# Moving the low part of the queries and the norm steps from VectorE to GpSimd, with half-height query loads and paired negations, in a fused attention and two-MLP kernel

## The chip, the cores and the metric

One core of one Trainium2 chip runs the whole program in one launch. The metric is device time in microseconds (us), the median over the runs. The engines have the names of the profile: PE is TensorE (PEld its weight loads), DVE is VectorE, ACT is ScalarE, POOL is GpSimd, and SP is SyncE, whose queue issues all of this kernel's DMAs.

## The reference

Inputs are q, k, v of shape (4, 12, 448, 64), so S = 448 and D = 64, and the weights of two feed-forward blocks over 1792 tokens of width 768.

```python
def rmsnorm(x, g):
    rms = np.sqrt(np.mean(x * x, axis=-1, keepdims=True) + 1e-06)
    return x / rms * g
q_n, k_n = rmsnorm(q, g_q), rmsnorm(k, g_k)
scores = (1.0 / np.sqrt(64)) * np.matmul(q_n, k_n.transpose(0, 1, 3, 2))
scores = scores - np.max(scores, axis=-1, keepdims=True)
attn = np.exp(scores)
attn = attn / (np.sum(attn, axis=-1, keepdims=True) + 1e-09)
x = np.matmul(attn, v)                # then heads side by side: (1792, 768)
x = ((x @ w1) * (x @ w2) @ w3) @ w_out
h = x @ w_in
out = (h * np.clip(h + 3.0, 0.0, 6.0) / 6.0) @ w_out2
```

## The kernel before, in words

The 48 heads are taken as 24 pairs (NP = 24). Everything is float32, and accuracy comes from splitting: a value is copied to the rounded type that PE multiplies quickly (the high part, on ACT), the rest is found by a subtraction (the low part, on DVE or POOL), and PE multiplies both.

A pair goes through attention in eight steps, one for each block of 112 queries (four) of each of its two heads. One turn of the main loop (lines 721 to 749) is one step. In step t it emits the two score matmuls of step t (L536, L537), the exponential of step t - 1 (`expo`, L555, ACT), the transposes of the exponentials of the pair before (`trans`, L562), their low part (`tlo`, L581, DVE), then `scale_max` (L543, DVE: scales the scores and takes the row maximum) and `negate` (L550, DVE: one column of the maximum times -1, as the bias of the exponential), the copy of the high part (`thi`, L571, ACT), and the product with the values (L602 to L615).

The queries of a pair are loaded twice, one copy above the other, into 128 partitions of the tile qr, 896 columns (`load_q`, one buffer). `qhi` (L505, ACT) scales all 128 rows by the product G of the two norm weights and writes the rounded result to the tile Q. `qlo` (L510, DVE) then turns rows 64 to 127 of Q into the low part: qr times G, less Q. `ksplit` writes the keys' high part on ACT (L516) and their low part on POOL (L517). The score matmul contracts over all 128 partitions, so high and low queries are summed in one pass.

The norms are taken for two pairs at a time. `ssq` (L436, ACT) squares, `ssum` (L442, DVE) adds up, `rms1` takes mean plus epsilon (L448, DVE) and then a logarithm and an exponential (L450, L451, ACT), and `rms2` does one Newton step and the factor 1/8 (L460 to L464 and L466, five small DVE instructions on 112 x 32 and 112 x 16). The result for the keys goes through two transposes and through HBM (rkd) to come back as a broadcast row (rb). At the end of a pair `rsum1` (L634, L635, DVE) inverts the sums, and `xout` (L639, POOL) multiplies the output by them once they are back from HBM as rsb.

Beside this run fillers, paced by `fill(*rate(t))`: first the product of w3 and w_out (to about 240 us), then the layers of the first feed-forward block. A preparation of weights feeds them: a load (raw), a conversion from the float64 bit pattern (L135 on ACT, L136, L138 and L141 on DVE), a high copy on ACT (L201, L285), and a low part on POOL (L203, L287), which frees the raw buffer for the next load. A part of a filler is placed behind the anchors of two or three steps ago (score, maximum and exponential).

The order on each engine is decided when the program is built: functions are entered at step times (lines 681 to 719, moved by SHIFT), and a scheduler with a modelled timeline orders the instructions. On the chip every engine and the SP queue then works strictly in that order.

Of the kernel before, what the change touches and what calls it, by code (L numbers as in the profile page):

```python
# [12 lines left out]
F32 = mybir.dt.float32  # L13
# [3 lines left out]
AF = mybir.ActivationFunctionType  # L17
ALU = mybir.AluOpType
# [4 lines left out]
B, H, S, D = 4, 12, 448, 64  # L23
HP = H // 2
NP = B * HP
P = 128
# [20 lines left out]
def fused_kernel(ctx: ExitStack, tc: tile.TileContext, nat, qT, kT, vin, gq, gk,  # L47
                 w12, w3t, wo, win, wo2, outT):
    nc = tc.nc
# [15 lines left out]
    G = gs[:, 2:3]  # L65
# [21 lines left out]
    def dma(out, src):  # L87
        return nc.sync.dma_start(out, src)
# [313 lines left out]
    T = {}  # L402
    anchors = {}

    def attention(ap, rate):
# [10 lines left out]
                    dma(T["nat", i], nat[i].rearrange("p a b d -> p (a b) d"))  # L416

        def load_q(i):
            T["qr", i] = ap.tile([P, 2, S], F32, tag="qr", bufs=1, name="qr")
            dma(T["qr", i], qT[i])  # L420

        def load_k(i):
            T["kr", i] = ap.tile([P, 2, S], F32, tag="kr", bufs=1, name="kr")
# [14 lines left out]
        def ssum(i, g):  # L438
            x = T.pop(("nat", i))
            if i == g[0]:  # L440
                T["ss", g[0]] = ap.tile([CP, 2, len(g), 2 * NC], F32, tag="ss", bufs=2, name="ss")
            nc.vector.reduce_sum(T["ss", g[0]][:, :, i - g[0], :],  # L442
                                 x.rearrange("p (a b) d -> p a b d", a=2), axis=AX.X)

        def rms1(g):
            w = 16 * len(g)
            v = T["ss", g[0]].rearrange("p a b c -> p (a b c)")
            nc.vector.tensor_scalar(v, v, 1.0 / D, 1e-6, op0=ALU.mult, op1=ALU.add)  # L448
            y = ap.tile([CP, w], F32, tag="ry", bufs=2, name="ry")
            nc.scalar.activation(y, v, AF.Ln)  # L450
            nc.scalar.activation(y, y, AF.Exp, scale=-0.5)  # L451
            T["ry", g[0]] = y

        def rms2(g):
            n = len(g)
            w = 16 * n
            v = T.pop(("ss", g[0])).rearrange("p a b c -> p (a b c)")
            y = T.pop(("ry", g[0]))
            t = ap.tile([CP, w], F32, tag="rt", bufs=2, name="rt")
            nc.vector.tensor_mul(t, y, y)  # L460
            nc.vector.tensor_mul(t, t, v)
            nc.vector.tensor_scalar(t, t, -0.5, 1.5, op0=ALU.mult, op1=ALU.add)
            r = ap.tile([CP, w], F32, tag="rr", bufs=2, name="rr")
            nc.vector.tensor_mul(r, y, t)  # L464
            rq = ap.tile([CP, n, 8], F32, tag="rq", bufs=3, name="rq")
            nc.vector.tensor_scalar_mul(rq, r[:, : 8 * n].rearrange("p (a b) -> p a b", b=8), 0.125)  # L466
            for i in g:
                T["rq", i] = rq[:, i - g[0], :]
            T["rr", g[0]] = r
# [32 lines left out]

        def qhi(i):
            T["Q", i] = q = ap.tile([P, 2, S], F32R, tag="Q", bufs=2, name="Q")
            nc.scalar.activation(q, T["qr", i], AF.Copy, scale=G)  # L505

        def qlo(i):
            a = slice(64, 128)
            q = T["Q", i]
            nc.vector.scalar_tensor_tensor(out=q[a], in0=T["qr", i][a], scalar=G[a, :], in1=q[a],  # L510
                                           op0=ALU.mult, op1=ALU.subtract)

        def ksplit(i):
            k1, k2 = T["K", i] = [ap.tile([P, 2, S], F32R, tag=f"K{z}", bufs=2, name="K") for z in range(2)]
# [12 lines left out]
        def score(i, s):  # L527
            j, c = divmod(s, NC)
            if s == 0:
                T["PP", i] = ap.tile([CP, NC, 2 * S], F32, tag="PP", bufs=2, name="PP")  # L530
                T["m", i] = ap.tile([CP, 16], F32, tag="mx", bufs=2, name="mx")
                T["sum", i] = ap.tile([CP, 8], F32, tag="sum", bufs=2, name="sum")
            k1, k2 = T["K", i]
            ps = bank("s")
            qs = T["Q", i][:, j, c * CP : c * CP + CP]
            nc.tensor.matmul(ps[:CP, :S], qs, k1[:, j, :], start=True, stop=False)  # L536
            anchors[8 * i + s] = [nc.tensor.matmul(ps[:CP, :S], qs, k2[:, j, :], start=False, stop=True)]  # L537
            return ps
# [8 lines left out]

        def negate(i, s):
            m = T["m", i]
            nc.vector.tensor_scalar_mul(m[:, 8 + s : 9 + s], m[:, s : s + 1], -1.0)  # L550

        def expo(i, s):
            j, c = divmod(s, NC)
            v = T["PP", i][:, c, j * S : j * S + S]
            anchors[8 * i + s].append(nc.scalar.activation(  # L555
                v, v, AF.Exp, bias=T["m", i][:, 8 + s : 9 + s], accum_out=T["sum", i][:, s : s + 1]))

        def trans(i, kb):
            src = T["PP", i]
            ps = bank("t")  # L560
            for c in range(NC):
                nc.tensor.transpose(ps[:, c * CP : c * CP + CP], src[:, c, kb * P : kb * P + P],  # L562
                                    ident[:CP, :CP])
            hi = ap.tile([P, S], F32 if full(i) else F32R, tag="xh", bufs=3, name="xh")
            lo = None if full(i) else ap.tile([P, S], F32R, tag="xl", bufs=3, name="xl")
            T["X", i, kb] = (ps[:, :S], hi, lo)
# [9 lines left out]
        def tlo(i, kb):  # L576
            ps, hi, lo = T["X", i, kb]
            if full(i):
                return
            if kb != 3 or i < K3:  # L580
                nc.vector.tensor_sub(lo, ps, hi)  # L581
            else:
                nc.vector.tensor_sub(hi[64:128, :], ps[0:64, :], hi[0:64, :])
                nc.vector.tensor_sub(lo[0:64, :], ps[64:128, :], lo[64:128, :])
# [96 lines left out]
        for i in range(NP):  # L681
            t = 8 * i
            n = i + 1
# [9 lines left out]
            if i % 2 == 0 and i + 2 < NP:  # L693
                g = groups[i + 2]
# [19 lines left out]
            if i % 2 == 0 and i + 2 < NP:  # L714
                g = groups[i + 2]
# [5 lines left out]
        t = -1  # L721
        while t < 8 * NP + 22 or xs_ready:
            t += 1
            if t == 4:
                first.close()
            now[0] = t
            live = t < 8 * NP
            ps = score(*divmod(t, 8)) if live else None
            if 0 < t <= 8 * NP:
                expo(*divmod(t - 1, 8))  # L730
            u = t - LG
            if 0 <= u < 8 * NP and u % 8 < 7:
                trans(*divmod(u, 8))
            if 0 <= u - 1 < 8 * NP and (u - 1) % 8 < 7:
                tlo(*divmod(u - 1, 8))
            if live:
                scale_max(t // 8, t % 8, ps)
                negate(*divmod(t, 8))
            if 0 <= u < 8 * NP and u % 8 < 7:
                thi(*divmod(u, 8))  # L740
            if 0 <= u - 2 < 8 * NP and (u - 2) % 8 < 7:
                pv(*divmod(u - 2, 8))
            with ExitStack() as es:
                for a in anchors.get(t - (3 if "pool" in L else 2), ()):
                    es.enter_context(tc.issue_after(a.ins))
                fill(*rate(t))
            run_tasks()
            if "pool" in L:
                xnext()

    def rate(t):
        if "pool" not in L:
            return 1.05, 2
        if L["cur"] < 8:
            return 2.5, 4
        return 1.6, 2
# [48 lines left out]
    step, q = 0, 0  # L805
# [33 lines left out]
    for b, t in enumerate(order):  # L839
        acc = None  # L840
        for m in range(M2):
# [26 lines left out]
            if acc is None:  # L868
# [4 lines left out]
                                           op0=ALU.min, op1=ALU.mult)  # L873
            g = lp.tile([P, 2, S], F32R, tag="g", bufs=2, name="g")
# [57 lines left out]
```

## Time and profile before

| what | value |
|---|---|
| median of 3 runs | 1273.02 us (1271.57 to 1277.7) |
| the profiled execution | 1276.18 us, span 1274.3 us |
| busy over the span | PE 93%, PEld 81%, DVE 62%, ACT 53%, POOL 36% |
| mean granted clock of PE | 0.968 of full |
| DMA | 203.72 MB, mean 160 GB/s |
| chain that ended last | PE 67%, DMA 11%, DVE 10%, issue 5%, ACT 3%, POOL 2% |

The shares are means over stages that differ: attention with the weight product, to about 240 us; attention with the first feed-forward block, to about 640 us; the rest of that block; and from about 870 us the second block alone, in which PE is busy throughout from 900 to 1200 us. So the stage tables, not the shares, say what a change in one stage is worth. In the rows, L12 is line 12 of the kernel, and a releaser behind an arrow is what ended the idle time of an engine.

### The profile page before, as it was taken

How to read it: one execution, taken by the hardware profiler on the slowest of the kernel's cores; microseconds unless marked ns; L12 is line 12 of the kernel's file. 1: busy time of each engine (PE TensorE's matmuls, PEld its weight loads, DVE VectorE, ACT ScalarE, POOL GpSimd, SP SyncE). 2: the span in 40 equal slices, each digit the busy share in tenths (PEclk: the TensorE clock that was granted, in tenths of full speed). 3: DMA queues.
4: the chain of work that ended last, by engine and by line, in shares of the span. 5: the costliest groups of instructions: out<-in, count | busy, mean ns of one | idle time of the engine just before them, and what ended most of it. 6: DMA issues, size and time to landing. Idle time of an engine off the chain costs nothing.

```text
span 1274.3 us, 16884 instructions
## 1 busy us (share of the span) xinstructions
PE 1183.1 (93%) x5868; PEld 1033.9 (81%) x5868; DVE 795.1 (62%) x1524; ACT 678.8 (53%) x1305; POOL 463.6 (36%) x292
## 2 busy tenths in 40 slices
PE   3587998888889999999999999889999999999998
PEld 2355987667668999999998998778999999999997
DVE  6989789989993578768643446994433343343332
ACT  5887667866783566766642223444533353344332
POOL 4334324624443112222111003445454454545542
PEclk9698998989999999999999999899999999999999
DMA  7898664666688666676349983450100020001001
GB/s 248 253 256 243 202 193 167 194 229 228 211 274 306 209 217 199 235 225 220 134 163 382 348 323 113 158 173 25 60 28 1 1 87 1 1 1 44 1 1 44
DMA packets 64693, 203.72 MB, mean 160 GB/s; under 512 B 8544, under 2 KB 25440, under 8 KB 64608
## 3 DMA queue, kind: packets, MB, share of 16 engines
q1 hardware_dynamic: 64608, 202.65, 48.2%
q8 instruction: 46, 0.75, 0.2%
q14 instruction: 39, 0.32, 0.1%
HBM read 173.93 MB, written 28.68 MB: 159 GB/s over the span
## 4 chain that ended last, share of the span: by engine, by line
PE 67%; DMA 11%; DVE 10%; issue 5%; ACT 3%; POOL 2%; SPq 1%; DVEq 0%; POOLq 0%; ACTq 0%
PE bank L80 8%; PE bank L82 8%; PE bank L81 8%; PE acc L81 6%; PE acc L82 6%; PE acc L80 5%; PE h L80 5%; PE h L81 5%; PE h L82 5%; PE bank L562 3%; DMA raw<-in_w_dram 2%; DVE wf L141 2%; DMA wr<-in_wo_dram 2%; PE bank L536 2%; PE bank L537 2%
## 5 line engine op out<-in xcount | busy, mean ns | idle before, releaser
L800 POOL TENSOR_TENSOR wis<-wf,wis 128x768 fp32r<-128x768 f32 x63 | 119.8, 1902 | 234.1 <-ACT wis L799 234.1
L872 DVE SCALAR_TENSOR_TENSOR u<-u,h 128x448 f32<-128x448 f32 x64 | 39.5, 618 | 217.3 <-ACT u L871 217.3
L800 POOL TENSOR_TENSOR wos<-wf,wos 128x768 fp32r<-128x768 f32 x64 | 119.0, 1860 | 103.6 <-ACT wos L799 103.6
L80 PE MATMUL bank<-xhl,ws 128*128 128x448 f32 x384 | 145.1, 378 | 7.7 <-ACT ws L285 6.3
L543 DVE CUSTOM_DVE_ANT_0 PP<-bank,rb,rq 112x448 f32<-112x448 f32 x192 | 129.1, 677 | 31.9 <-PE bank L537 27.4
L82 PE MATMUL bank<-xhl,ws 128*128 128x448 f32 x384 | 143.9, 375 | 4.9 <-POOL ws L287 4.9
L81 PE MATMUL acc<-g,wos 128*128 128x448 f32 x384 | 144.3, 376 | 3.8 <-DVE g L876 3.7
L555 ACT ACTIVATE PP<-PP,mx 112x448 f32<-112x448 f32 x192 | 127.4, 664 | 37.4 <-DVE mx L550 34.2
L80 PE MATMUL acc<-g,wos 128*128 128x448 f32 x384 | 138.5, 371 | 5.5 <-ACT g L875 5.5
L82 PE MATMUL acc<-g,wos 128*128 128x448 f32 x384 | 143.2, 373 | 0.0
L81 PE MATMUL bank<-xhl,ws 128*128 128x448 f32 x384 | 142.5, 371 | 0.1
L80 PE MATMUL h<-x2h,wis 128*128 128x448 f32 x378 | 139.0, 368 | 0.0
L81 PE MATMUL h<-x2h,wis 128*128 128x448 f32 x378 | 138.9, 368 | 0.0
L82 PE MATMUL h<-x2h,wis 128*128 128x448 f32 x378 | 137.5, 364 | 0.4 <-POOL wis L800 0.4
L876 DVE TENSOR_TENSOR g<-u,g 128x448 fp32r<-128x448 f32 x64 | 97.9, 1529 | 33.6 <-ACT g L875 33.6
L871 ACT ACTIVATE u<-h,half 128x448 f32<-128x448 f32 x64 | 40.4, 631 | 143.2 <-PE h L82 143.2
L536 PE MATMUL bank<-K,Q 128*112 128x448 f32 x192 | 78.3, 409 | 37.5 <-DVE mx L543 25.0
L562 PE MATMUL bank<-ident,PP 112*128 112x112 f32 x672 | 97.0, 267 | 11.8 <-DVE xl L581 10.2
L562 PEld LDWEIGHTS bank<-ident,PP 112*128 112x128 f32 x672 | 80.5, 145 | 33.8 <-DVE xl L581 13.3
L571 ACT ACTIVATE xh<-bank 128x448 fp32r<-128x448 f32 (+1 forms) x156 | 83.0, 537 | 43.3 <-PE bank L562 38.4
L581 DVE TENSOR_TENSOR xl<-bank,xh 128x448 fp32r<-128x448 f32 x142 | 87.1, 615 | 25.5 <-ACT xh L571 23.8
L799 ACT ACTIVATE wos<-wf 128x768 fp32r<-128x768 f32 x64 | 54.1, 846 | 86.9 <-PE acc L82 86.7
(126 smaller groups left out, 2763.5 us busy)
## 6 DMA issues: line engine op xcount, KB each, us to landing
ws<-w12d SPq DMA_DIRECT2D x48, 768.0 KB, 5.1
ws<-wpd SPq DMA_DIRECT2D x32, 768.0 KB, 4.2
raw<-in_w_dram SPq DMA_DIRECT2D x32, 384.0 KB, 4.3
w12d<-ws SPq DMA_DIRECT2D x16, 768.0 KB, 6.0
wr<-in_win_dram SPq DMA_DIRECT2D x16, 768.0 KB, 4.5
wr<-in_wo_dram SPq DMA_DIRECT2D x16, 768.0 KB, 6.6
nat<-in_nat_dram SPq DMA_DIRECT2D x24, 448.0 KB, 5.9
qr<-in_qT_dram SPq DMA_DIRECT2D x24, 448.0 KB, 6.4
```

The costliest lines, as they stand in the source:

```text
L80: nc.tensor.matmul(ps, lh, rh, start=first, stop=False)
L81: nc.tensor.matmul(ps, lh, rl, start=False, stop=False)
L82: return nc.tensor.matmul(ps, ll, rh, start=False, stop=last)
L536: nc.tensor.matmul(ps[:CP, :S], qs, k1[:, j, :], start=True, stop=False)
L543: anchors[8 * i + s].append(nc.vector.tensor_tensor_reduce(out=T["PP", i][:, c, sl], in0=ps[:CP, :S], in1=T["rb", i][:, sl], op0=ALU.mult, ...
L555: anchors[8 * i + s].append(nc.scalar.activation(v, v, AF.Exp, bias=T["m", i][:, 8 + s : 9 + s], accum_out=T["sum", i][:, s : s + 1]))
L562: nc.tensor.transpose(ps[:, c * CP : c * CP + CP], src[:, c, kb * P : kb * P + P], ident[:CP, :CP])
L571: nc.scalar.activation(hi, ps, AF.Copy)
L581: nc.vector.tensor_sub(lo, ps, hi)
L799: nc.scalar.activation(t[:, 0, :], wf[q], AF.Copy)
L800: nc.gpsimd.tensor_sub(t[:, 1, :], wf[q], t[:, 0, :])
L876: nc.vector.tensor_sub(g[:, 1, :], u, g[:, 0, :])
```

## The change

Four edits. The queries are loaded to 64 partitions, scaled there in place by ACT, and copied to the upper half of Q by a second ACT instruction; the low part is a POOL subtraction. The six small steps of `rms1` and `rms2` run on POOL for every group but the first. `negate` works in odd steps only, on two columns. The exponential of step t - 2, not t - 1, is emitted in step t.

```diff
         def load_q(i):
-            T["qr", i] = ap.tile([P, 2, S], F32, tag="qr", bufs=1, name="qr")
-            dma(T["qr", i], qT[i])
+            T["qr", i] = ap.tile([D, 2, S], F32, tag="qr", bufs=1, name="qr")
+            dma(T["qr", i], qT[i][:D])
...
+        def eng(g):
+            return nc.gpsimd if g[0] else nc.vector
+
         def rms1(g):
...
-            nc.vector.tensor_scalar(v, v, 1.0 / D, 1e-6, op0=ALU.mult, op1=ALU.add)
+            eng(g).tensor_scalar(v, v, 1.0 / D, 1e-6, op0=ALU.mult, op1=ALU.add)
...
-            nc.vector.tensor_mul(t, y, y)
-            nc.vector.tensor_mul(t, t, v)
-            nc.vector.tensor_scalar(t, t, -0.5, 1.5, op0=ALU.mult, op1=ALU.add)
+            eng(g).tensor_mul(t, y, y)
+            eng(g).tensor_mul(t, t, v)
+            eng(g).tensor_scalar(t, t, -0.5, 1.5, op0=ALU.mult, op1=ALU.add)
             r = ap.tile([CP, w], F32, tag="rr", bufs=2, name="rr")
-            nc.vector.tensor_mul(r, y, t)
+            eng(g).tensor_mul(r, y, t)
             rq = ap.tile([CP, n, 8], F32, tag="rq", bufs=3, name="rq")
-            nc.vector.tensor_scalar_mul(rq, r[:, : 8 * n].rearrange("p (a b) -> p a b", b=8), 0.125)
+            eng(g).tensor_scalar_mul(rq, r[:, : 8 * n].rearrange("p (a b) -> p a b", b=8), 0.125)
...
         def qhi(i):
             T["Q", i] = q = ap.tile([P, 2, S], F32R, tag="Q", bufs=2, name="Q")
-            nc.scalar.activation(q, T["qr", i], AF.Copy, scale=G)
+            qr = T["qr", i]
+            nc.scalar.activation(qr, qr, AF.Copy, scale=G[:D, :])
+            nc.scalar.activation(q[:D], qr, AF.Copy)
 
         def qlo(i):
-            a = slice(64, 128)
             q = T["Q", i]
-            nc.vector.scalar_tensor_tensor(out=q[a], in0=T["qr", i][a], scalar=G[a, :], in1=q[a],
-                                           op0=ALU.mult, op1=ALU.subtract)
+            nc.gpsimd.tensor_sub(q[D:], T["qr", i], q[:D])
...
         def negate(i, s):
             m = T["m", i]
-            nc.vector.tensor_scalar_mul(m[:, 8 + s : 9 + s], m[:, s : s + 1], -1.0)
+            if s % 2:
+                nc.vector.tensor_scalar_mul(m[:, 7 + s : 9 + s], m[:, s - 1 : s + 1], -1.0)
...
-            if 0 < t <= 8 * NP:
-                expo(*divmod(t - 1, 8))
+            if 1 < t <= 8 * NP + 1:
+                expo(*divmod(t - 2, 8))
```

## Rows read from the trace of the kernel before

**Rows 1.** Stretches: length, busy PE, PEld, DVE, ACT, POOL (count), clock, DMA share, GB/s.
```profile
40.00:400.00 360.00, 305.76 (x1500) 243.79 (x1499) 320.68 (x767) 263.16 (x574) 150.99 (x109) 0.91 0.72 223
...
400.00:480.00 80.00, 80.00 (x434) 72.64 (x433) 43.43 (x104) 41.41 (x87) 11.53 (x8) 1.00 0.67 225
```

**Rows 2.** The longest wait of PE, 40 to 400 us: total us, times, longest us.
```profile
PE bank L536 <- DVE mx L543: 20.9, 12, 5.8
```

**Rows 3.** Groups on DVE, 40 to 400 us: busy us, mean ns | idle before.
```profile
L510 DVE SCALAR_TENSOR_TENSOR Q<-qr,gs,Q 64x896 fp32r<-64x896 f32 x14 | 23.2, 1660 | 2.5 <-ACT Q L505 2.1
...
L550 DVE TENSOR_SCALAR mx<-mx 112x1 f32<-112x1 f32 x107 | 14.9, 142 | 0.4
...
L460 DVE TENSOR_TENSOR rt<-ry 112x32 f32<-112x32 f32 x11 | 5.1, 464 | 0.1
L462 DVE TENSOR_SCALAR rt<-rt 112x32 f32<-112x32 f32 x11 | 4.8, 439 | 0.0
...
L448 DVE TENSOR_SCALAR ss<-ss 112x32 f32<-112x32 f32 x10 | 3.1, 308 | 0.0
...
L461 DVE TENSOR_TENSOR rt<-rt,ss 112x32 f32<-112x32 f32 x11 | 2.9, 261 | 0.1
...
L466 DVE TENSOR_SCALAR rq<-rr 112x16 f32<-112x16 f32 x9 | 2.3, 257 | 0.0
```

**Rows 4.** The same stretch, line L464 alone: its busy us and count.
```profile
40.00:400.00 360.00, 2.11 (x9) 0.91 0.72 223
```

**Rows 5.** The chain that ended last, to 420 us: start us, us, what.
```profile
41.79 1.15 DVE Q L510
43.02 1.84 issue
...
53.20 1.82 DVE rt L462
...
181.73 2.17 issue
...
203.45 2.44 issue
...
360.86 1.16 DVE Q L510
```

**Rows 6.** Timelines of DVE and of POOL: start us, us, what, idle before.
```profile
181.70 2.17 DVE L510 SCALAR_TENSOR_TENSOR Q<-qr,gs,Q 64x896 fp32r<-64x896 f32 x1 [1.83 <-ACT Q L505]
...
180.80 2.12 POOL L517 TENSOR_TENSOR K<-kr,K 128x896 fp32r<-128x896 f32 x1 [7.77 <-ACT K L516]
```

**Rows 7.** Single lines of the whole run: duration ns least/median/longest, first and last start.
```profile
L510 DVE SCALAR_TENSOR_TENSOR Q<-qr,gs,Q x24: 1150/1635/3026, 10.1 to 595.6; 64x896 fp32r<-64x896 f32 x24
...
L550 DVE TENSOR_SCALAR mx<-mx x192: 130/147/156, 22.4 to 640.4; 112x1 f32<-112x1 f32 x192
...
L634 DVE TENSOR_SCALAR sum<-sum x24: 151/172/1244, 44.9 to 641.4; 112x8 f32<-112x8 f32 x24
...
L141 DVE SCALAR_TENSOR_TENSOR raw<-raw x64: 535/556/1634, 14.6 to 383.4; 128x384 int32<-128x384 int32 x48, 128x512 int32<-128x512 int32 x16
```

**Rows 8.** More groups, 40 to 400 us: POOL and ACT, then DVE.
```profile
L517 POOL TENSOR_TENSOR K<-kr,K 128x896 fp32r<-128x896 f32 x14 | 31.2, 2232 | 22.8 <-ACT K L516 15.9 <-DMA nat<-in_nat_dram 6.8
L141 DVE SCALAR_TENSOR_TENSOR raw<-raw 128x384 int32<-128x384 int32 x44 | 31.2, 709 | 0.2
...
L516 ACT ACTIVATE K<-kr 128x896 fp32r<-128x896 f32 x14 | 13.2, 944 | 0.4 <-PE bank L536 0.4
...
L634 DVE TENSOR_SCALAR sum<-sum 112x8 f32<-112x8 f32 x14 | 5.4, 384 | 0.0
```

**Rows 9.** Waits of POOL, then of the SP queue, 40 to 400 us.
```profile
POOL xs L639 <- DMA rsb<-rsd: 19.4, 5, 5.6
...
SPq L88 <- DVE Q L510: 23.0, 9, 10.5
```

**Rows 10.** The smallest POOL instruction of its start-up with a tile in and out.
```profile
masks.py:199 POOL TENSOR_SCALAR_AFFINE_SELECT ident<-ident 128x128 f32<-128x128 f32 x1 | 0.3, 292 | 0.1
```

## The prediction

> **What bounds the kernel now.** I read the stage table first, then who PE waits for, then the groups of DVE, and last the chain that ended last. The stage table [rows 1] cuts the run in two. From 400 to 480 us PE is busy 80.00 of 80 us at a granted clock of 1.00, while DVE, ACT and POOL have room: there, nothing that relieves DVE is worth anything, and nothing that loads POOL costs anything. Before that, from 40 to 400 us, PE is busy 305.8 of 360 us at a mean clock of 0.91, and DVE 320.7, or 89%. POOL is busy 151 us, or 42%. So DVE is the fullest engine of this stretch, and the waits agree: PE's longest there is for DVE, 20.9 us for a score bank that the maximum has not left [rows 2]. All that follows is about these 360 us; what comes after is only shifted.
>
> In the groups of DVE [rows 3, 4] the reader is to see what the change touches: `qlo` with 23.2 us, the negations with 14.9 us, and the six norm steps with 5.1 + 4.8 + 3.1 + 2.9 + 2.3 + 2.1 = 20.3 us. Their means are far over their bare times: `qlo` takes 1150 ns at least, 1635 in the median and 3026 at most [rows 7]. The chain [rows 5] passes through these lines. `qlo` stands on it eight times, from 41.79 to 360.86 us, with 9.8 us. Two "issue" pieces, 2.17 and 2.44 us, are also `qlo`: on the timeline the instruction begun at 181.70 us lasts just those 2.17 us, a full 1.02 over its least; POOL's subtraction of the keys, begun before it at 180.80 us, ends inside it at 182.92 [rows 6]. The norm steps stand there 24 times, most of them with 0.1 us, in all with 5.2; the 1.82 us of L462 are the longest, and the 1.84 us of issue at 43.02 belong to L460. That is 14.4 us of `qlo` and 7.1 of norm steps: 21.5 of the 43.5 us that they use, 49%. One half is what I take as the part of DVE time in this stretch that turns into time.
>
> **The change part by part.** The sum is made against the profiled execution's own 1276.2 us, which is 3.2 us above the median of 1273.0.
>
> *Low queries and norm steps leave DVE.* 23.2 + 20.3 = 43.5 us less on DVE, and half of it is **-21.7 us**. The first group stays on DVE and ran before 40 us, so it is not in the count.
>
> *Paired negations.* 107 become some 53. A one-column negation takes 147 ns in the median and never more than 156 in 192 [rows 7]. No row has two columns. The nearest of the same kind is L634, eight columns: 151 ns at least but 1244 at most [rows 7], and 384 in the mean of this stretch [rows 8]. The lower end is 147 ns each, 7 us less than before; the upper end is every one at 1244, 66 us, 51 more. I take L634's mean, since it differs only in columns, and let its waiting part of 0.23 us grow with POOL's load (below, by a third) to 0.30: 53 x 0.45 = 24 us, **9 us more on DVE** and not less.
>
> *Longer waits of what stays.* POOL gains one subtraction of 896 columns per pair. The row of the keys' subtraction gives 2232 ns [rows 8]; 64 partitions instead of 128 could lie at half of that, the other bound; I take 2.2, since nothing shows POOL faster on fewer rows: 14 x 2.2 = 31 us. It gains six norm steps for ten groups. The smallest instruction with a tile in and out took 0.29 us [rows 10], the lower bound; the subtraction's 2.2 us is the upper. I take 0.3: 18 us. So POOL goes from 151 to 200 us, a third more. Some DVE instructions already run long: L141 has a mean of 709 ns [rows 8] against a median of 556 in the run [rows 7], 6.7 us of waiting in 44 instructions. With L138 and L136, as many each, and a few others I put it at some 22 us; a third more is **7 us**. Bounds are nothing and 22.
>
> Half of these 9 + 7 us gives back **+8 us**.
>
> *PE's clock.* The gaps that PE waits through also cost clock: 0.91 instead of 1.00 over 305.8 us is at most 27.5 us. PE idles 54.2 us; the 13.7 us saved so far are 25% of that, and 25% of 27.5 is **-7 us** (bounds: nothing, and all of it).
>
> *Second ACT instruction of `qhi`.* By the keys' copy of equal width it takes 0.944 us [rows 8], 14 of them 13 us. ACT is idle 97 of the 360 us [rows 1], which covers it; of 13 `qhi` the chain holds two, so **+2 us**, bounds 0 and 13. If that cover goes, exponentials come late next.
>
> *Later exponentials.* Emitted a step later, they have a step less before the transposes of the next pair. PE's longest wait in this stretch is not for an exponential [rows 2], and its work on the pair at hand hides the delay: cost nothing. If that cover is gone, the price is at most one step of the eight once per pair.
>
> *Queue of SP.* The load of the next queries waits until `qlo` has read the one buffer: 23.0 us over nine waits [rows 9], with keys, raw weights and norms' inputs queued behind. On POOL `qlo` shares the engine with the keys' subtraction, so it ends up to 2.2 us later: between 0 and 31 us of SP time. By the step times of the code what is loaded then is scaled five steps later, so I take **+2 us**. The halved load saves 224 of 448 KB a pair, a twenty-fifth of what moves at 223 GB/s: **-1 us**. At the start ACT has a second instruction ahead of the first exponential of the norms: **+1 us**.
>
> Sum: -21.7 + 8 - 7 + 2 + 2 - 1 + 1 = -16.7, so 1259.5 for this execution, and with 3.2 taken off, **1256 us** in the median.
>
> **The rivals.** *The port takes it back (20%).* An instruction of DVE drags while a subtraction of POOL runs [rows 6], and the longest `qlo`, L141 and L634 [rows 7] look the same. If every negation of two columns is caught as the worst L634 was, DVE gets 51 us there and 22 from the other waits against 43.5 saved. At half of both, 36.5 against 43.5, DVE is about where it was: -7, half of it on the path, so **1270 us** in the median. I take this middle for the rival. For it: one column was never caught and eight columns were. Against: L634's median of 172 ns says that most are not. [...]
>
> *POOL's queue becomes the wait (23%, slower).* ACT's logarithm will wait for POOL's first norm step, and POOL works in order: that step can stand behind a running subtraction (2.2 us, half of it in the mean) and behind `xout`, which waits for its row from HBM, 19.4 us over five waits in this stretch and 5.6 at the longest [rows 9], 1.6 us per pair. Behind the waiting logarithm on ACT stand exponentials and high parts, for which DVE and PE wait. At 1.1 + 1.6 = 2.7 us for ten groups it is 27 us; on the path in full, -16.7 + 27 gives 1286.5 less 3.2, **1283 us**. It decides from 1.7 us per group, where the 16.7 are gone. For it: nothing of POOL is waited for by ACT's norms now. Against: POOL idles 58%, and ACT's 97 idle us can take half.
>
> *More than forecast (12%).* If DVE time turns into time in full, 43.5 - 16 = 27.5 us, with the clock's share doubled to 14, and with nothing else lost: -41, or **1232 us**. PE's own rate after 400 us, 434 instructions in 80 us, would need 277 us for these 1500, so PE allows it.
>
> That the order changes by more than the change says is possible in each case, as the scheduler orders the whole program anew.
>
> **How the numbers follow.** The forecast has 45%, and with half of each bound its own range is 1246 to 1267. It and the last case (12%) are faster by over 0.5%, that is below 1266.7, 0.5% being about what a measurement of this kernel can tell from no change: 0.57. The port's case lies within: 0.20. POOL's queue is slower: 0.23. The range leaves out about half of the last case and half of the queue's, some 18%, and reaches just over the queue's middle: 1238 to 1283.
>
> **What would show it.** Right: in 40 to 400 us, or the stretch that holds the same work, DVE near 295 us busy, POOL near 200, PE's wait for L543 down, clock above 0.91, and the first stage with PE full beginning some 17 us earlier. Negations of two columns would have a longest of 1 to 2 us and a mean near 0.45. Wrong: ACT waiting for POOL at L450, SP waiting for POOL's `qlo` much over 23 us, PE waiting for exponentials, or the saving lost again after 400 us.

## The result, and the profile after

The changed kernel takes 1290.29 us in the median of four runs (1288.63 to 1292.3) against 1273.49 us for the kernel before in runs beside them: 1.0131 times [1.0111, 1.015], or **16.8 us slower**. The forecast was 1256 us with a range up to 1283; it was wrong in sign, and the result lies above the range. The profiled execution of after has a span of 1289.2 us against 1274.3, and a mean clock of 0.964 against 0.968.

The stretches of the kernel after, in the columns of [rows 1]; the last row adds up the whole run:

```profile
40.00:400.00 360.00, 294.55 (x1424) 234.61 (x1424) 311.62 (x626) 267.05 (x577) 188.67 (x177) 0.89 0.70 208
400.00:480.00 80.00, 80.00 (x433) 72.44 (x431) 38.70 (x89) 42.33 (x89) 26.26 (x21) 1.00 0.72 232
...
sum 1289.00, PE 1186.21 PEld 1038.10 DVE 781.69 ACT 693.13 POOL 532.76; mean PE 237.24 PEld 207.62 DVE 156.34 ACT 138.63 POOL 106.55
```

The same last row of the kernel before:

```profile
sum 1289.00, PE 1183.06 PEld 1033.88 DVE 795.12 ACT 678.76 POOL 463.57; mean PE 236.61 PEld 206.78 DVE 159.02 ACT 135.75 POOL 92.71
```

From 40 to 400 us PE got through 1424 instructions instead of 1500 and its clock fell from 0.91 to 0.89. From 400 to 480 us it is as full as before. Taken instruction by instruction, the delay against before comes and goes: the 300th matmul is 15 us late, the 700th 6, the 1500th, which before starts at 390 us, 17, the 2200th 17 and the last 15. So all of the loss stands at 400 us and is only carried after that. DVE was relieved, but by 9.1 us in this stretch (320.7 to 311.6) where 27.5 were forecast, and by 13.4 us in the whole run.

PE's waits from 40 to 400 us, after: total us, times, longest us.

```profile
PE bank L566 <- DVE xl L585: 21.5, 10, 5.2
PE bank L539 <- DVE mx L546: 15.5, 14, 3.7
PE bank L566 <- ACT xh L575: 4.4, 2, 3.4
PE bank L618 <- ACT xh L575: 3.2, 2, 1.6
PE bank L539 <- POOL Q L514: 3.1, 1, 3.1
```

In the kernel before, the first of these was:

```profile
PE bank L562 <- DVE xl L581: 10.2, 8, 3.3
```

The wait for the maximum fell from 20.9 [rows 2] to 15.5 us, but the wait of the transposes for a bank that the low part (`tlo`, L585) has not left rose from 10.2 to 21.5. The two together rose from 31.1 to 37.0 us: PE waits for DVE more than before, in another place.

The groups on DVE in the same stretch of the kernel after (busy us, mean ns | idle before):

```profile
L138 DVE SCALAR_TENSOR_TENSOR raw<-raw 128x384 int32<-128x384 int32 x45 | 38.1, 851 | 0.5 <-ACT raw L135 0.5
L141 DVE SCALAR_TENSOR_TENSOR raw<-raw 128x384 int32<-128x384 int32 x45 | 35.2, 785 | 0.3
...
L554 DVE TENSOR_SCALAR mx<-mx 112x2 f32<-112x2 f32 x52 | 24.5, 471 | 0.1
...
L141 DVE SCALAR_TENSOR_TENSOR raw<-raw 128x512 int32<-128x512 int32 x14 | 16.4, 1171 | 0.1
L138 DVE SCALAR_TENSOR_TENSOR raw<-raw 128x512 int32<-128x512 int32 x14 | 12.7, 904 | 0.6 <-ACT raw L135 0.6
```

The three groups of conversions of the kernel before that [rows 8] did not show:

```profile
L138 DVE SCALAR_TENSOR_TENSOR raw<-raw 128x384 int32<-128x384 int32 x44 | 30.7, 697 | 0.2
...
L138 DVE SCALAR_TENSOR_TENSOR raw<-raw 128x512 int32<-128x512 int32 x13 | 10.8, 828 | 1.3 <-ACT raw L135 1.3
L141 DVE SCALAR_TENSOR_TENSOR raw<-raw 128x512 int32<-128x512 int32 x14 | 10.1, 724 | 0.0
```

With L141's 31.2 us of [rows 8], L138 and L141 took 82.8 us for 115 instructions before and take 102.4 for 118 now. L136 did not grow: 31.7 us for 56 before, 29.5 for 57 now. Two columns are negated in 471 ns, so 52 of them use 24.5 us, where 107 single ones used 14.9 [rows 3].

Three single lines of the kernel after over the whole run, in the columns of [rows 7], show that this is waiting and not longer work:

```profile
L138 DVE SCALAR_TENSOR_TENSOR raw<-raw x64: 509/559/2678, 12.5 to 396.6; 128x384 int32<-128x384 int32 x48, 128x512 int32<-128x512 int32 x16
...
L141 DVE SCALAR_TENSOR_TENSOR raw<-raw x64: 535/559/2560, 15.3 to 397.2; 128x384 int32<-128x384 int32 x48, 128x512 int32<-128x512 int32 x16
...
L554 DVE TENSOR_SCALAR mx<-mx x96: 120/169/2090, 28.8 to 657.3; 112x2 f32<-112x2 f32 x96
```

L141's median is 559 ns as against 556 before, but its longest is 2560 instead of 1634 [rows 7]; the negation's median is 169 ns and its longest 2090. What they wait for stands on the timelines of the first 15 us, DVE above, POOL below:

```profile
10.23 2.20 DVE L136 TENSOR_SCALAR raw<-raw 128x512 int32<-128x512 int32 x1 [1.55 <-DMA raw<-in_w3t_dram]
12.54 2.37 DVE L138 SCALAR_TENSOR_TENSOR raw<-raw 128x512 int32<-128x512 int32 x1
14.83 0.18 DVE L463 TENSOR_TENSOR rt<-ry 112x32 f32<-112x32 f32 x1
14.94 0.42 DVE L136 TENSOR_SCALAR raw<-raw 128x512 int32<-128x512 int32 x1
15.27 0.68 DVE L141 SCALAR_TENSOR_TENSOR raw<-raw 128x512 int32<-128x512 int32 x1
...
10.06 2.08 POOL L520 TENSOR_TENSOR K<-kr,K 128x896 fp32r<-128x896 f32 x1 [8.76 <-ACT K L519]
12.22 2.14 POOL L514 TENSOR_TENSOR Q<-qr,Q 64x896 fp32r<-64x896 f32 x1
```

The conversion begun at 10.23 us lasts 2.20 us and the same one begun at 14.94 lasts 0.42. The first ends 0.3 us after the keys' subtraction on POOL, and the next, begun at 12.54, 0.5 us after the new subtraction of the queries. L463, the first step of the Newton iteration of the norms, stands behind both.

The same rows show that the durations of neighbours overlap: L136 of 14.94 us lasts until 15.36, and L141 starts at 15.27. The groups add up durations, while busy time counts an overlap once. Added up one by one, DVE's instructions from 40 to 400 us take 371.4 us before and 353.2 after, 18.2 less; the overlap is 50.7 us in 767 instructions before and 41.6 in 626 after. That is why busy time falls by 9.1 only.

What moved to POOL and ACT, 40 to 400 us (POOL's two, then ACT's three), and a wait of the SP queue, 0 to 400 us:

```profile
L514 POOL TENSOR_TENSOR Q<-qr,Q 64x896 fp32r<-64x896 f32 x13 | 28.4, 2187 | 4.2 <-ACT Q L510 3.4
...
L464 POOL TENSOR_TENSOR rt<-rt,ss 112x32 f32<-112x32 f32 x11 | 4.9, 445 | 0.6
...
L509 ACT ACTIVATE qr<-qr,gs 64x896 f32<-64x896 f32 x14 | 14.5, 1035 | 2.6 <-DMA qr<-in_qT_dram 2.4 <-POOL rt L464 0.2
L510 ACT ACTIVATE Q<-qr 64x896 fp32r<-64x896 f32 x14 | 13.2, 941 | 0.0
...
SPq L88 <- POOL Q L514: 21.7, 11, 4.9
```

The six norm steps take 306 to 478 ns each on POOL. Among the waits from 40 to 400 us no wait of ACT for POOL's first norm step (L451) appears.

### The profile page after: what moved, and what is told of

Its sections match the earlier page's. It is cut to its first block, busy times and chain, and to the rows that moved or that the text cites. A ratio compares the mean times of both kernels' runs of the same rounds, so it can differ in the third digit from the quotient of the medians.

```text
span 1289.2 us, 16814 instructions
## 1 busy us (share of the span) xinstructions
PE 1186.2 (92%) x5868; PEld 1038.1 (81%) x5868; DVE 781.7 (61%) x1338; ACT 693.1 (54%) x1329; POOL 532.8 (41%) x382
## 4 chain that ended last, share of the span: by engine, by line
PE 66%; DMA 11%; DVE 10%; issue 4%; POOL 4%; ACT 4%; SPq 1%; POOLq 0%; DVEq 0%; ACTq 0%
PE bank L80 8%; PE bank L82 8%; PE bank L81 8%; PE acc L81 5%; PE acc L82 5%; PE acc L80 5%; PE h L80 5%; PE h L81 5%; PE h L82 5%; PE bank L566 3%; DVE wf L141 2%; PE bank L539 2%; DMA wr<-in_wo_dram 2%; PE bank L540 2%; DMA raw<-in_w3t_dram 2%
## 5 line engine op out<-in xcount | busy, mean ns | idle before, releaser
L566 PE MATMUL bank<-ident,PP 112*128 112x112 f32 x672 | 99.7, 272 | 26.4 <-DVE xl L585 21.5
L585 DVE TENSOR_TENSOR xl<-bank,xh 128x448 fp32r<-128x448 f32 x142 | 86.8, 615 | 32.7 <-ACT xh L575 32.2
L575 ACT ACTIVATE xh<-bank 128x448 fp32r<-128x448 f32 (+1 forms) x156 | 82.1, 536 | 30.4 <-PE bank L566 29.4
```

What stands on the lines that cost most here:

```text
L575: nc.scalar.activation(hi, ps, AF.Copy)
```

## The experiments

In the expectations P is the prediction's first rival, that beside POOL's subtractions DVE loses what it was relieved of ("port" is its name there; no run shows one), C that the start sets the loss, S that the exponentials and negations come too late, N that norm steps in POOL's queue hold ACT, A and L that ACT's added time counts in full, F that ACT has room, and R that the instruction order does it; each text says what it expects. Ratios are to the kernel before in runs beside each, which had medians of 1273.1 to 1274.6 us.

### One part undone in the kernel after

**undo_q**: the queries as before (full load, one ACT instruction, low part on DVE), the rest as after.

```diff
-            qr = T["qr", i]
-            nc.scalar.activation(qr, qr, AF.Copy, scale=G[:D, :])
-            nc.scalar.activation(q[:D], qr, AF.Copy)
+            nc.scalar.activation(q, T["qr", i], AF.Copy, scale=G)
...
-            nc.gpsimd.tensor_sub(q[D:], T["qr", i], q[:D])
+            nc.vector.scalar_tensor_tensor(out=q[a], in0=T["qr", i][a], scalar=G[a, :], in1=q[a],
+                                           op0=ALU.mult, op1=ALU.subtract)
```

> The changed kernel with the queries as before (128-partition load, one ACT instruction, low part on VectorE); norms on GpSimd and paired negations stay. [...] By P the first maximum is back at 21 to 23 us, the mean of the conversion's 128x384 instructions falls from 0.85 and 0.79 us towards 0.70, and the time falls by 8 to 14 us, to 1276 to 1282. Theory S (lateness: exponentials a step later and negation by pairs tie ACT and the fillers closer to the maxima): the time stays within 4 us of 1290. Theory N (norm steps on GpSimd's queue hold ACT): stays within 4 us of 1290.

Measured: 1276.69 us, 1.0019 [1.0, 1.0038], inside what P expected. Nearly all of the loss is gone.

**undo_pairs**: one-column negations, exponential of step t - 1.

```diff
-            if s % 2:
-                nc.vector.tensor_scalar_mul(m[:, 7 + s : 9 + s], m[:, s - 1 : s + 1], -1.0)
+            nc.vector.tensor_scalar_mul(m[:, 8 + s : 9 + s], m[:, s : s + 1], -1.0)
...
-            if 1 < t <= 8 * NP + 1:
-                expo(*divmod(t - 2, 8))
+            if 0 < t <= 8 * NP:
+                expo(*divmod(t - 1, 8))
```

> The changed kernel with one-column negations and the exponential of step t - 1 as before; queries and norms stay as changed. Theory P: negations no longer wait (0.15 us instead of 0.47 in the mean), 10 us less of VectorE before 400 us, half on the path: 1283 to 1287, and the first maximum stays at 27 us. Theory S: most of the loss is here, 1272 to 1279. Theory N: 1290 as it is.

Measured: 1294.65 us, 1.0153 [1.0127, 1.0179]; P and S both expected less than 1290. The negations take 14.5 us again (x107, 140 ns), 10.0 less than in after, but DVE as a whole is not relieved from 40 to 400 us, 312.3 us against 311.6:

```profile
40.00:400.00 360.00, 294.19 (x1437) 232.23 (x1436) 312.26 (x692) 269.73 (x580) 194.35 (x180) 0.90 0.69 207
```

L136 grew to 41.3 us for 56 instructions, and the eight-column step of `rsum1` from 6.7 to 13.2 us for 14: other instructions wait instead.

**undo_norms**: all norm steps on DVE.

```diff
-            return nc.gpsimd if g[0] else nc.vector
+            return nc.vector
```

> The changed kernel with all norm steps on VectorE; queries and negations stay as changed. Theory P: GpSimd loses 25 us of small instructions before 400 us, VectorE gains 15 to 25 of them back, partly stuck behind the subtractions: within 5 us of 1290, either way. Theory S: the same. Theory N: ACT's logarithm waits no more and the time falls by 8 us or more, to 1282 or less.

Measured: 1304.51 us, 1.0233 [1.0195, 1.027], 14 us above after, where every theory expected 5 us either way or less time. The same steps cost DVE 33.3 us here (L464 alone 7.1 us, 648 ns each) instead of the 20.3 of before. It follows that the queries' part carries the loss, and that the other two do not add up with it: undoing the norms' part makes it worse, and undoing the pairs changes nothing clear of the spread (its interval overlaps that of after).

### The start

The first maximum of after comes at 27.5 us, before at 21.2. **q0_vector** puts the first pair's low part on DVE; **pair0_before** gives the first pair its queries wholly as before.

```diff
-            nc.gpsimd.tensor_sub(q[D:], T["qr", i], q[:D])
+            (nc.gpsimd if i else nc.vector).tensor_sub(q[D:], T["qr", i], q[:D])
```

> The changed kernel with the low part of the first pair's queries alone on VectorE (a subtraction there, from the new 64-partition tile). Theory P: the first maximum comes back to 21 to 24 us, and the time falls by 3 to 6 us, to 1284 to 1287. Theories S and N: the start is made up for later, since the stage to 400 us is bound elsewhere, and the time stays at 1288 to 1292.

Measured: 1296.42 us, 1.017 [1.0142, 1.0199]; the first maximum stays at 27.3 us, so this run does not test what it was made for.

```diff
+            if i == 0:
+                nc.scalar.activation(q, qr, AF.Copy, scale=G)
+                return
...
+            if i == 0:
+                nc.vector.scalar_tensor_tensor(out=q[a], in0=T["qr", i][a], scalar=G[a, :], in1=q[a],
+                                               op0=ALU.mult, op1=ALU.subtract)
+                return
```

> The changed kernel with the first pair's queries handled as before (full load, one ACT instruction, low part on VectorE); the other 23 pairs as changed. Theory C: the first maximum is back at 21 to 23 us and the time at 1276 to 1282. Theory P: the start comes back, but 22 later subtractions before the end of attention stay: 1283 to 1289. Theory A: the same as P.

Measured: 1291.03 us, 1.0137 [1.0109, 1.0165], with the first maximum at 21.5 us. The 6 us of the start came back and the end did not move: the 300th matmul is 5.5 us late, the 1500th 17 again. The start is not the cause.

### The queries' part taken to pieces

**extra_pool** and **extra_act** add to undo_q an idle instruction per pair, as large as one of those the queries' part adds; **tiny_pool** and **tiny_act** add the same with 8 columns.

```diff
+            nc.gpsimd.tensor_sub(T["qr", i][D:], T["qr", i][:D], q[:D])
```

> Undo_q (queries as before, norms on GpSimd, paired negations; 1276.7) with one more GpSimd subtraction of 64 x 896 per pair, into rows of the loaded queries that are dead by then; only the next load waits for it. It does no useful work. Theory P (the subtraction on GpSimd is the price, through what it holds back on VectorE and on its own queue): 1284 to 1292, and the conversion's means on VectorE grow to 0.8 us or more. Theory A (the second ACT instruction is the price): 1276 to 1280. Theory C (the order of the first 30 us is the price): 1276 to 1281.

Measured: 1291.34 us, 1.0144 [1.0118, 1.0169].

```diff
+            nc.scalar.activation(T["qr", i][:D], T["qr", i][:D], AF.Copy)
```

> Undo_q (1276.7) with one more ACT copy of 64 x 896 per pair, in place on rows that are dead by then; only the next load waits for it. It does no useful work. Theory A: 1284 to 1292. Theories P and C: 1276 to 1281, since ACT is idle a quarter of the stretch to 400 us.

Measured: 1290.68 us, 1.0135 [1.0099, 1.0171].

The stretch from 40 to 400 us of undo_q, of extra_pool and of extra_act, in the columns of [rows 1]:

```profile
40.00:400.00 360.00, 303.71 (x1504) 240.20 (x1505) 320.61 (x665) 264.82 (x581) 168.32 (x168) 0.92 0.71 223
```

```profile
40.00:400.00 360.00, 297.89 (x1443) 233.30 (x1442) 339.65 (x644) 257.80 (x565) 195.09 (x178) 0.91 0.70 215
```

```profile
40.00:400.00 360.00, 296.90 (x1425) 233.44 (x1424) 314.07 (x640) 267.78 (x577) 162.48 (x165) 0.88 0.70 216
```

In extra_pool, 14 idle subtractions take POOL 31.4 us, and DVE works 19 us longer than in undo_q (339.65 against 320.61) without an instruction of its own more: the price of what POOL holds up. It falls on the paired negations above all, which take 22 us more (undo_q, then extra_pool):

```profile
L554 DVE TENSOR_SCALAR mx<-mx 112x2 f32<-112x2 f32 x55 | 15.9, 288 | 0.1
...
L555 DVE TENSOR_SCALAR mx<-mx 112x2 f32<-112x2 f32 x53 | 38.1, 718 | 0.2
```

In extra_act DVE is not busier, and yet as much is lost. Each of the two alone costs what the whole queries' part costs in the change, though there DVE also loses the 23.2 us of `qlo`.

```diff
+            nc.scalar.activation(T["qr", i][:D, 0, :8], T["qr", i][:D, 0, :8], AF.Copy)
```

> Undo_q (1276.7) with one more ACT copy per pair as in extra_act, but of 8 columns instead of 896: some 0.2 us instead of 0.93, in the same place of the program. Theory L (each instruction more on ACT, or each wait more inside VectorE, lengthens the loops between the engines about in full, so the price goes with the added time: 16 pairs to 400 us x 0.93 = 15 us for extra_act): 1277 to 1281. Theory R (the price is that of another order of all instructions, which any addition brings about): 1284 to 1295.

Measured: 1280.77 us, 1.0047 [1.0028, 1.0065].

```diff
+            nc.gpsimd.tensor_sub(T["qr", i][D:, 0, :8], T["qr", i][:D, 0, :8], q[:D, 0, :8])
```

> Undo_q (1276.7) with one more GpSimd subtraction per pair as in extra_pool, but of 8 columns: some 0.3 us instead of 2.1, in the same place. Theory L: 1276 to 1280. Theory R: 1284 to 1295.

Measured: 1277.41 us, 1.0029 [1.0014, 1.0045]. An instruction of 0.2 us per pair costs 4 and 1 us over undo_q, the 4 barely clear of the spread and the 1 within it: most of the 14 goes with the length, as L expected.

**qlo_vector** leaves in the kernel after the two ACT instructions and takes the subtraction off POOL; **no_scale** leaves out the scaling by G, so that ACT has one instruction.

```diff
-            nc.gpsimd.tensor_sub(q[D:], T["qr", i], q[:D])
+            nc.vector.tensor_sub(q[D:], T["qr", i], q[:D])
```

> The changed kernel with the low part of all queries on VectorE (a subtraction from the 64-partition tile); half load, two ACT instructions, norms on GpSimd and paired negations stay. Theory P: 1274 to 1281. Theory A: 1285 to 1292, as the changed kernel. Theory C: 1282 to 1287, since ACT still delays the norm steps of the first group.

Measured: 1295.5 us, 1.0168 [1.0134, 1.0202].

```diff
-            qr = T["qr", i]
-            nc.scalar.activation(qr, qr, AF.Copy, scale=G[:D, :])
-            nc.scalar.activation(q[:D], qr, AF.Copy)
+            nc.scalar.activation(q[:D], T["qr", i], AF.Copy)
```

> The changed kernel without the scaling of the queries by the product of the norm weights, which is left out: one ACT instruction instead of two per pair, the low part still on GpSimd from the half load. Theory L: the 15 us of ACT go, VectorE's relief stays and GpSimd's holds stay: 1272 to 1282. Theory R: nothing is said, anything from 1275 to 1295.

Measured: 1282.5 us, 1.0069 [1.0049, 1.0089]. Taking POOL's subtraction away gives nothing, against what P expected (1274 to 1281); taking one ACT instruction away gives 8 of the 17 us. That spoke for ACT's time.

### Parts alone in the kernel before

**only_q** makes the queries' part alone; **no_square** tests the mirror of ACT's theory by taking the squares of the norms (L436) off ACT after the first group (the first norm step of those groups then gives a constant, an edit not shown).

```diff
-            nc.scalar.activation(q, T["qr", i], AF.Copy, scale=G)
+            qr = T["qr", i]
+            nc.scalar.activation(qr, qr, AF.Copy, scale=G[:D, :])
+            nc.scalar.activation(q[:D], qr, AF.Copy)
...
+            nc.gpsimd.tensor_sub(q[D:], T["qr", i], q[:D])
```

> The kernel before with the queries' part of the change alone (half load, two ACT instructions, low part on GpSimd); norms on VectorE, negations of one column. Theory L: ACT's 15 us and GpSimd's holds against 23 us less of VectorE: 1284 to 1296. Theory R: 1284 to 1300, too, since the order changes; what tells L and R apart are the runs beside it.

Measured: 1292.22 us, 1.0149 [1.0118, 1.018].

```diff
-            nc.scalar.activation(x, x, AF.Square)
+            pass
```

> The kernel before without ACT's squares for the norms after the first group (22 instructions of 1.05 us; the squaring is left out, and the first norm step gives a constant so that all values stay finite). It takes about 1 us per pair off ACT, as much as the change put on. Theory L (ACT's time before 400 us counts about in full although ACT is idle a quarter of it): 1257 to 1266, 8 to 16 us less. Rival F (ACT has room, and the runs with more on ACT were slower through their order): 1269 to 1277.

Measured: 1267.58 us, 0.9955 [0.9922, 0.9988]. ACT's theory wanted 8 to 16 us back and got 6, its rival F 5 at most: the run decides for neither. An idle ACT instruction added costs in full (14 us for 13.1), and 22 squares left out, 23.2 us of ACT and all before 400 us, give back 6: what an instruction costs is not a property of the engine's time alone.

**half_load** halves the load and the partitions that `qhi` and `qlo` read, with as many instructions on every engine; **half_norms** adds the norms on POOL, **only_norms** has them alone.

```diff
-            nc.scalar.activation(q, T["qr", i], AF.Copy, scale=G)
+            nc.scalar.activation(q[:D], T["qr", i], AF.Copy, scale=G[:D, :])
...
-            nc.vector.scalar_tensor_tensor(out=q[a], in0=T["qr", i][a], scalar=G[a, :], in1=q[a],
+            nc.vector.scalar_tensor_tensor(out=q[D:], in0=T["qr", i], scalar=G[:D, :], in1=q[:D],
```

> The kernel before with the half load alone: one ACT instruction on 64 rows, the same VectorE instruction for the low part, read from the lower rows. Theory L: neither engine has more or less to do, only 224 KB per pair less to load: 1269 to 1275. Rival F: the same, and a loss of 5 us or more here would put the price of the queries' part on the half load.

Measured: 1279.92 us, 1.0041 [1.0021, 1.0061].

```diff
-            nc.vector.tensor_mul(t, y, y)
+            eng(g).tensor_mul(t, y, y)
```

(and so for the other five steps)

> half_load with the six norm steps of every group but the first on GpSimd: VectorE is relieved of 20 us and GpSimd holds it for about 20 more in short pieces, ACT has no more to do. Theory L: 1264 to 1274. If norm steps on GpSimd hold ACT: 1278 or more.

Measured: 1288.14 us, 1.0111 [1.0085, 1.0136], where L expected 1274 at most.

> The kernel before with the norm steps alone on GpSimd. Theory L: 1266 to 1275, since ACT has no more to do and VectorE less. If norm steps on GpSimd hold ACT: 1278 or more.

Measured: 1280.84 us, 1.0049 [1.003, 1.0068], where L expected 1275 at most. Both lie where the texts put norm steps that hold ACT, but the waits of ACT for a norm step on POOL come to less than 2 us in either run, so that is not it. Norm steps on POOL cost 6 us alone and 8 on top of the half load, and in the kernel after they are worth 14 (undo_norms): the same edit with either sign, by what stands beside it. half_load moves fewer bytes and adds no work, and is slower by about 5 us. Its text would put the price of the queries' part on the half load then; the trace shows another order: its first maximum comes at 26.1 us instead of 21.2, as DVE's order now has the first group's norm steps behind conversions. That the rest of its loss is order too is argued, since no engine has more to do. So an edit costs or gains by the order that it leads to, and under this ordering rule no kernel tried is faster than before, but for one that leaves work out; undo_q is level with it.

### The ordering rule

**before_plain** and **after_plain** are the two kernels with the scheduler's modelled timeline switched off. The functions, the step times and the work are the same: DVE runs 1524 instructions in both versions of before and 1338 in both of after, PE 5868 matmuls in all four.

```diff
-    with _tile.TileContext(nc, schedule_with_timeline_sim=True) as tc:
+    with _tile.TileContext(nc, schedule_with_timeline_sim=False) as tc:
```

> The kernel before with the scheduler's modelled timeline turned off, so that its instructions are ordered by another rule. Both theories: slower than 1274, since the step times were chosen with the timeline, 1276 to 1340; it is the base for after_plain.

Measured: 1251.47 us (1246.61 to 1252.24), 0.9822 [0.9794, 0.9849]. Both theories expected it slower than before.

> The changed kernel ordered by the same other rule. Theory L (the work costs: ACT's second instruction, GpSimd's subtraction in the way of VectorE): 8 to 25 us slower than before_plain. Theory R (the loss of 17 us was the order): within 6 us of before_plain, or faster.

Measured: 1253.59 us (1251.99 to 1255.63), 0.9848 [0.9821, 0.9876].

Before gains 22 us, after 37 (1290.29 to 1253.59). Between the two now lie 2.1 us instead of 16.8, and their intervals overlap; R had expected 6 at most, L 8 to 25. **before_plain has the best time measured, ahead of both kernels of this case.** Its stretches, and PE's longest waits from 40 to 400 us:

```profile
40.00:400.00 360.00, 321.59 (x1630) 263.01 (x1631) 319.82 (x761) 265.50 (x579) 153.08 (x109) 0.94 0.72 235
...
sum 1289.00, PE 1172.41 PEld 1029.69 DVE 802.90 ACT 678.95 POOL 462.16; mean PE 234.48 PEld 205.94 DVE 160.58 ACT 135.79 POOL 92.43
```

```profile
PE bank L562 <- DVE xl L581: 6.9, 7, 2.2
...
PE bank L536 <- DVE mx L543: 0.8, 1, 0.8
```

The same two views of after_plain:

```profile
40.00:400.00 360.00, 317.15 (x1602) 255.17 (x1603) 312.01 (x632) 271.22 (x586) 192.71 (x172) 0.94 0.71 223
...
sum 1289.00, PE 1168.90 PEld 1024.79 DVE 780.68 ACT 693.93 POOL 529.01; mean PE 233.78 PEld 204.96 DVE 156.14 ACT 138.79 POOL 105.80
```

```profile
PE bank L566 <- DVE xl L585: 7.1, 7, 1.5
PE bank L539 <- DVE mx L546: 3.1, 4, 1.1
```

DVE is as busy as under the other rule (319.8 and 312.0 against 320.7 and 311.6), but PE does 1630 and 1602 instructions in the stretch, and its waits for the maximum are all but gone. One place shows what the orders do, the beginning of the fifth pair. In after, PE makes its first score at 118.24 us, and this is what DVE does (a row of PE, then rows of DVE, then one of POOL):

```profile
118.24 0.45 PE L539 MATMUL bank<-K,Q 128*112 128x448 f32 x1
...
126.57 2.62 DVE L138 SCALAR_TENSOR_TENSOR raw<-raw 128x512 int32<-128x512 int32 x1
130.11 1.31 DVE L136 TENSOR_SCALAR raw<-raw 128x512 int32<-128x512 int32 x1 [0.92 <-DMA raw<-in_w3t_dram]
131.34 1.77 DVE L141 SCALAR_TENSOR_TENSOR raw<-raw 128x512 int32<-128x512 int32 x1
...
140.75 0.43 DVE L136 TENSOR_SCALAR raw<-raw 128x512 int32<-128x512 int32 x1 [2.39 <-DMA raw<-in_w3t_dram]
...
146.89 0.68 DVE L546 CUSTOM_DVE_ANT_0 PP<-bank,rb,rq 112x448 f32<-112x448 f32 x1
...
126.06 2.58 POOL L520 TENSOR_TENSOR K<-kr,K 128x896 fp32r<-128x896 f32 x1
```

The maximum that empties this bank starts 28.7 us after its score. From 122.45 us on, eleven conversions of 12.3 us in all stand between, beside low parts and sums of squares. Five of the eleven are drawn out to more than 1 us, as the one begun at 126.57 is beside the keys' subtraction on POOL; two wait for a load, 0.92 and 2.39 us; and DVE takes them all before the maximum. In after_plain the same pair:

```profile
125.35 0.36 PE L539 MATMUL bank<-K,Q 128*112 128x448 f32 x1
...
126.45 0.68 DVE L546 CUSTOM_DVE_ANT_0 PP<-bank,rb,rq 112x448 f32<-112x448 f32 x1
```

1.1 us. Summed over the pairs 1 to 13, from a pair's first score to its first maximum: 119 us in before, 150 in after, 40 in before_plain, 20 in after_plain. That is a reading of one symptom, not an account of the loss: undo_q has 123 and extra_pool 121, though 15 us lie between those two.

## Why the prediction was wrong, point by point

**The step that failed** is the first term, -21.7 us: "half of 43.5" taken as the part of DVE time that turns into time. Three things in it did not hold.

*Durations were taken for busy time.* The 43.5 us are durations of groups, and they were taken off a busy time of 320.7. Part of each duration overlaps the neighbour's: the durations of all groups together fell by 18.2 us, the busy time by 9.1, since with 141 fewer instructions 9.1 us of overlap went too. The prediction has no term for this.

*Of the DVE time, most came back as waits.* Off DVE went the 43.5 us, back came 9.6 for the paired negations (9 forecast, 471 ns against 450 taken; but the same instruction takes 288 ns in undo_q and 718 in extra_pool, so the match is in part luck) and some 18 for L138 and L141 alone (102.4 less 82.8, less two for three more instructions), where 7 were taken and 22 was the bound for all longer waits. L320, at 1155 ns instead of 652, is another. This is the first rival, and it has the place right: DVE's instructions last longer beside POOL's. Its 7 us less on DVE are close to the 9.1 measured, in part by luck, as it has no overlap either and put most of the waits on the negations; its 1270 us is 20 under the result. On the first timeline L136 begins 0.17 us after POOL's subtraction on 128 partitions and ends 0.29 after it, 2.20 us for an instruction of 0.42; L138 begins 0.32 us after the subtraction on 64 partitions and ends 0.55 after it, 2.37 us where the next of its form, at 15.98 us, takes 0.68. The negations show the same on the timelines of the whole run. After, 25 of the 96 of two columns last over 0.25 us, each with at least 88% of its time beside an instruction of POOL; 55 of the other 71 have none beside them. Before, 42 of the 180 of one column that stand on a row of their own run beside one for more than half their time, and no negation is longer than 156 ns [rows 7]. Why two columns are held up where one is not, no run shows.

*What was saved did not turn into time.* With the model off, DVE's sum over the whole run falls from 802.9 to 780.7 us, by 22, and the kernel is not faster but 2.1 us slower within the spread. So the share of one half, read off the chain, is no rate of exchange that holds from one order to the other. undo_pairs can't test it under the first rule: its negations take 10 us less, but DVE as a whole is as busy as in after. Under the other rule the change's work is about neutral, near the small gain of 3 us that the first rival gave it.

**Beyond that, the order.** The other 15 us, 16.8 less 2.1, are in no rival. The prediction said that the scheduler orders the whole program anew, and priced it at nothing. The last pair of runs shows that the loss hangs on the order: the same edits, ordered by the other rule, cost 2 us. It also shows that the price of a step was read in an order that was already 22 us from a better one; from 40 to 400 us PE's wait for the maximum is 20.9 us in it and 0.8 in the other. What remains argued and not shown is how much of the 14 to 18 us that the queries' part costs there (13.6 from undo_q to after, 18.4 from before to only_q) is work falling on a place without slack, and how much is other placement. Placement alone, in edits with little or no work, cost 1 to 5 us under the first rule (tiny_pool, tiny_act, half_load); the rest goes with the length of what was added. Which single placement costs what was not found. Nor was an idle instruction put into the other order, so that there is room for it there is not shown by itself.

*Second ACT instruction, +2 (bounds 0 and 13).* An idle one of 938 ns costs 14.0 us (undo_q to extra_act), and leaving one out of after gives 7.8. The upper bound was near the truth in this order, although ACT is busy only 267 of 360 us. That ACT's 97 idle us cover it was the mistake: the idle time lies elsewhere than the instruction. In after, ACT stands idle 3.40 us before the weight copy (L221) of 145.36 us, and the high part behind it (L575), whose transposes had ended by 144.51, starts only at 145.75.

*Half load, -1.* Alone it is +5 us, with fewer bytes and no more work.

*POOL.* 2187 ns for the subtraction (2.2 taken), 306 to 478 ns for norm steps (300 taken, a little low), 188.7 us busy (200). *SP queue:* 21.7 us for POOL's low part from 0 to 400 us, beside 23.0 for DVE's before [rows 9], all of it from 40 us on: no more than before, where +2 was taken. *POOL's queue as the wait:* ACT's logarithm does not wait for POOL; this rival gave 1283 us, the nearest to the result, for a wait that did not come. *Clock:* it went down with PE's idle time, 0.91 to 0.89, so the sign of that term followed the first. *After 400 us* nothing changed, as said. *The later exponentials* were costed at nothing, and undo_pairs, which takes them back with the pairs, gains nothing; no run takes them back alone.

## What to carry to other kernels

Before a change of engines is priced on a kernel whose instruction order a scheduler makes, run the old kernel under another ordering rule: the 22 us found here were more than the change itself was worth in either order, and the price of the change moved from 16.8 to 2.1 us. Look at how long after its matmul the consumer of a PE bank starts; where a queue of conversions stands between, another order may be worth more than relief of the engine. Take busy time off busy time, not a group's added durations. And a move from VectorE to GpSimd must be charged for those VectorE instructions that a GpSimd instruction holds up, here the conversions of L138 and L141 (82.8 to 102.4 us) and, once widened to two columns, the negations (14.9 to 24.5): 31.4 us of idle subtractions cost VectorE 19.

## What was not expected of the hardware

- Widening the negation from one column to two raised its mean from 142 to 471 ns and its longest from 156 to 2090, so that half as many instructions took 24.5 us instead of 14.9. In undo_q the mean is 288 ns, in extra_pool 718.
- POOL's subtraction of 896 columns takes 2187 ns on 64 partitions and 2207 on 128 (L514 and L520 after): half the partitions save 20 ns.
- A norm step on 112 x 32 takes 234 to 464 ns in the mean on DVE before [rows 3, 4], 306 to 445 on POOL, and up to 648 back on DVE in undo_norms.
